# A fused attention and gated convolution: sums for two sets of scales in the free columns of the score tiles, fewer plain fp32 pairs, and a new order

## The chip, the cores and the metric

The kernel runs on one core of a Trainium2 chip. The metric is the device time of one execution in microseconds (us). The kernel before takes 588.35 us, the median of three runs (588.15 to 589.11). The core has five engines that run their own queues in order and wait for each other by semaphores: TensorE (PE, matmuls into PSUM), VectorE (DVE), ScalarE (ACT), GpSimd (POOL) and SyncE (SP, which issues the DMAs).

## The reference

```python
scores = scale * np.matmul(q, k.transpose(0, 1, 3, 2)) - np.log(S)   # q, k, v: 8 x 12 x 448 x 64
attn = 1.0 / (1.0 + np.exp(-scores))
x = np.matmul(attn, v)                           # then 8 x 448 x 768, heads side by side
gate_pre[t] = sum(conv_w[k] * xp[t + k] for k in range(5))   # xp: x with 4 zero tokens ahead
gate = 1.0 / (1.0 + np.exp(-gate_pre))
out = (gate * (x @ w_val)) @ w_out               # w_val, w_out: 768 x 768
```

All is fp32. There is no softmax: each score goes through a sigmoid alone.

## The kernel before, in words

**Units.** A *pair* is two heads of one batch (48 pairs, number i), a *two* is two pairs (24 twos, number j), and three twos are a batch. Tokens stand in the free dimension: a tile of scores has keys on its partitions and 448 queries beside each other, one half for each head. The first three chunks of 128 keys of a pair are `scores` (lines 497 to 510), the last 64 keys of both pairs of a two are one tile, `scores_rest` (512). Score tiles are `ps_a`, a ring of three PSUM buffers of two 512-wide halves, of which the scores fill columns 0 to 447. `attend` (575) multiplies the sigmoids by v, again into a `ps_a` tile, which becomes x.

**Plain and split.** A fp32 product on PE is either plain, or split into high and low parts with three cheaper matmuls (high·high and the two mixed ones). For the scores, pairs in `WHOLE_SCORES` are plain and the others have q and k split by `split_qk` (`qk_hi` by ACT or DVE, `qk_lo` by POOL). For the attend, twos in `WHOLE` are plain (`a_single`); for the others the sigmoid is written back into PSUM (line 541), ACT makes the fp16 high part `a`, DVE the low part (line 552), and v is split by a scale that is found from its maximum: a maximum on DVE (`vm`), a sum over partitions by a one-column matmul against ones (line 525), read by DVE (`v_exp`, line 533), four small DVE steps and `v_hi`, `v_lo`.

**Batches.** Batch 0's x goes to DRAM, and 64 of its tokens are appended to each of batches 1 to 7, which so have 512 tokens. For each of them: `x_max` (line 642) per two, the convolution (`gate`, 655: a first tap and four more per pair, then a sigmoid), and when its third two is done `x_scale` (664): DVE reduces `x_max`, spreads it on a 128x128 `diagonal` (673), PE sums that against ones into a `ps_m` tile (675), DVE reads it back (676) and makes a power-of-two scale, after which `x_split` makes the fp16 parts `xs`. `product` (704) makes for each of six output columns a chain of 18 fp16 matmuls of 512 columns (line 719): "val" (here V0 to V5) gives y, gated by DVE (743) and split into `g`; "out" (O0 to O5) takes the `g` and goes to the output. `ps_m` is a ring of two 512-wide PSUM buffers; two products run interleaved. One batch's O follow after the next batch's scale.

**Weights.** They come as 64-bit words and are turned into fp32 by DVE and ACT (`convert`), and then split to fp16 by `weight_split` (411): a sum of one column on PE (414) into a `ps_m` tile, small DVE steps (`exponent`, 386), a high part (361) and a low part (429) for each of 6 columns of each weight. `EARLY` = 5 columns of w_out are split while the first batch is attended, the last one with batch 1's products.

**Order.** A planner (129 to 246) takes all operations with a due time, worked out from the numbers in `AT` (74), and writes each engine's queue: of the ready operations the one with the earliest due time goes first. Chains with `then` (a pair's three chunks, an attend) stay together on PE. DVE and POOL aren't put side by side where they share an operand port.

## Time and profile before

| | us |
|---|---|
| three runs, median (lowest to highest) | 588.35 (588.15 to 589.11) |
| the profiled execution's own time | 587.99 |
| its span in the trace | 586.2 |
| PE busy in the span | 577.5 |
| DVE busy | 454.4 |
| ACT busy | 373.1 |
| POOL busy | 69.4 |

So 1.8 us of an execution lie outside the span. The busy times are sums over the whole span; how close an engine is to its limit in one stage is read from windows. The chain of waits follows the work that ended last back to the start, and each of its rows gives the start, the length and the line of one stretch on it. Start times are from the start of the span.

### The profile page before, as it was taken

Reading aid. Unit: us, or ns where it says so; the run is one execution under the profiler, and the core shown is the slowest. Engines: PE = TensorE matmul, PEld = TensorE weight load, DVE = VectorE, ACT = ScalarE, POOL = GpSimd, SP = SyncE. Lnnn points to the kernel's source line nnn. Section 1 sums busy time; section 2 is a strip of 40 time slices with the busy share of each in tenths; the row PEclk is TensorE's granted clock in tenths of the full one; section 3 lists DMA queues with packets and bytes.
Section 4 is the critical chain, followed back from the end, with each engine's and each line's share of the span. In section 5 each row is a group of like instructions: output and inputs, shape, how many; then the busy total and the mean of one; then the engine's idle time right before and its main releaser. Section 6 shows DMA issues by size and latency. Waiting matters only on the chain.

```text
span 586.2 us, 9120 instructions
## 1 busy us (share of the span) xinstructions
PE 577.5 (99%) x3509; PEld 274.6 (47%) x3509; DVE 454.4 (78%) x744; ACT 373.1 (64%) x495; POOL 69.4 (12%) x86
## 2 busy tenths in 40 slices
PE   8999999999999999999999999999999999999997
PEld 4333333444554455554545455455454544444444
DVE  1889999989978899889999789996899964813210
ACT  6678768646787677877767677687776762321111
POOL 0000020032110311112121131210111000100000
PEclk9999999999999999999999999999999999999999
DMA  8997633213232121431213322043220111021012
GB/s 314 394 335 227 215 102 123 49 61 126 53 115 71 74 96 37 130 101 47 95 25 124 90 75 66 30 130 95 67 85 0 37 42 36 2 72 37 0 37 72
DMA packets 30811, 56.94 MB, mean 97 GB/s; under 512 B 14000, under 2 KB 19632, under 8 KB 30768
## 3 DMA queue, kind: packets, MB, share of 16 engines
q1 hardware_dynamic: 30768, 56.37, 29.1%
q8 instruction: 27, 0.44, 0.3%
q14 instruction: 16, 0.13, 0.1%
HBM read 43.96 MB, written 12.40 MB: 96 GB/s over the span
## 4 chain that ended last, share of the span: by engine, by line
PE 85%; DVE 12%; ACT 2%; issue 1%; ACTq 0%; DVEq 0%
PE ps_m L719 54%; PE ps_a L506 13%; PE ps_a L599 12%; DVE gate L655 3%; PE ps_a L528 3%; PE ps_a L591 2%; DVE w_words L381 1%; ACT a_single L541 1%; DVE w_words L404 1%; DVE x_max L642 1%; DVE y L743 1%; DVE out_max L407 1%; DVE w_out_lo L429 1%; PE ps_m L766 1%; ACT y L359 1%
## 5 line engine op out<-in xcount | busy, mean ns | idle before, releaser
L719 PE MATMUL ps_m<-g,w_out_hi 128*128 128x512 f16 (+1 forms) x516 | 150.5, 374 | 1.6 <-ACT y L359 0.7
L719 PE MATMUL ps_m<-xs,w_val_hi 128*128 128x512 f16 x504 | 150.0, 379 | 1.0 <-DVE y L743 0.4
L655 DVE SCALAR_TENSOR_TENSOR gate<-x,cw,gate 128x512 f32<-128x512 f32 x168 | 123.2, 760 | 0.2
L552 DVE SCALAR_TENSOR_TENSOR a<-ps_a,a 128x896 f16<-128x896 f32 x84 | 88.9, 1084 | 12.5 <-ACT a L359 12.3
L719 PE MATMUL ps_m<-g,w_out_lo 128*128 128x512 f16 (+1 forms) x258 | 96.5, 374 | 0.0
L719 PE MATMUL ps_m<-xs,w_val_lo 128*128 128x512 f16 x252 | 95.5, 379 | 0.0
L541 ACT ACTIVATE ps_a<-ps_a 128x896 f32<-128x896 f32 x98 | 86.5, 904 | 9.5 <-DVE v_exp L533 5.9
L364 POOL TENSOR_TENSOR qk_lo<-qk_src,qk_hi 128x448 fp32r<-128x448 f32 (+1 forms) x52 | 61.8, 1209 | 249.8 <-ACT qk_hi L353 201.7
L719 PEld LDWEIGHTS <-w_val_hi 128*128 128x128 f16 x504 | 48.0, 98 | 63.6 <-issue 8.6
L719 PEld LDWEIGHTS <-w_out_hi 128*128 128x128 f16 x516 | 49.3, 98 | 60.7 <-issue 6.1
L359 ACT ACTIVATE a<-ps_a 128x896 f16<-128x896 f32 x84 | 74.3, 924 | 0.3
L359 ACT ACTIVATE y<-ps_m,o_scale 128x512 f32<-128x512 f32 (+1 forms) x39 | 26.0, 682 | 60.6 <-PE ps_m L719 59.8
L541 ACT ACTIVATE a_single<-ps_a 128x896 f32<-128x896 f32 x70 | 59.6, 924 | 7.5 <-PE ps_a L591 3.6
L743 DVE SCALAR_TENSOR_TENSOR y<-ps_m,y_scale,gate 128x512 f32<-128x512 f32 x42 | 30.1, 744 | 34.8 <-PE ps_m L719 32.6
L506 PE MATMUL ps_a<-qk_single 64*128 64x448 f32 x264 | 55.4, 554 | 0.0
L359 ACT ACTIVATE gate<-x,cw 128x512 f32<-128x512 f32 x38 | 27.6, 730 | 36.8 <-DVE y L743 36.8
L599 PE MATMUL ps_a<-a_single,v_src 128*64 128x448 f32 x240 | 47.3, 543 | 0.0
L599 PE MATMUL ps_a<-a,v_hi 128*64 128x448 f16 x336 | 46.1, 354 | 0.0
L658 ACT ACTIVATE gate<-gate 128x512 f32<-128x512 f32 x42 | 26.0, 628 | 25.2 <-DVE gate L655 25.1
L719 PEld LDWEIGHTS <-w_out_lo 128*128 128x128 f16 x258 | 25.2, 98 | 29.2
L719 PEld LDWEIGHTS <-w_val_lo 128*128 128x128 f16 x252 | 24.6, 98 | 29.8
L506 PEld LDWEIGHTS ps_a<-qk_single 64*128 64x128 f32 x264 | 23.8, 187 | 25.5 <-issue 17.1
(105 smaller groups left out, 641.0 us busy)
## 6 DMA issues: line engine op xcount, KB each, us to landing
qk_src<-qk SPq DMA_DIRECT2D x26, 448.0 KB, 3.8
v_src<-vs SPq DMA_DIRECT2D x24, 448.0 KB, 3.3
qk_single<-qk SPq DMA_DIRECT2D x21, 448.0 KB, 4.9
out_t<-y SPq DMA_DIRECT2D x41, 224.0 KB, 2.0
w_words<-w_val SPq DMA_DIRECT2D x6, 768.0 KB, 10.2
w_words<-w_out SPq DMA_DIRECT2D x6, 768.0 KB, 6.2
x<-first_x SPq DMA_DIRECT2D x21, 68.0 KB, 2.3
first_x<-x_first SPq DMA_DIRECT2D x3, 452.0 KB, 5.6
```

Source lines behind the costliest of these rows:

```text
L359: nc.scalar.activation(to, x, AF.Copy, scale=by)
L364: engines[eng].tensor_tensor(to, x, y, op=ALU.subtract)
L506: mm(b()[:, h, :S], k()[rows, at : at + P], q()[rows, :S], start=(n == 0), stop=(n == len(terms(i)) - 1))
L528: mm(b()[to, h, :S], x[n]()[rows, CW:], x[n]()[rows, :S], start=True, stop=True)
L541: nc.scalar.activation(to, b()[:, :, :S], AF.Sigmoid, bias=-math.log(S), scale=1.0 / math.sqrt(D))
L552: op({"V": 1.0}, t + 0.5, lambda e: nc.vector.scalar_tensor_tensor(part(1), p(), A_SCALE, part(0), op0=ALU.mult, op1=ALU.subtract), [b], [ ...
L591: mm(px()[to, p, :S], v()[rows, h * D : (h + 1) * D], x(s["a"])[rows, h, at : at + S], start=(n == 0), stop=False, skip_group_check=True)
L599: mm(px()[to, p, :S], v()[:, o : o + D], x(st[2 * j + p]["a", c])[:, h, at : at + S], start=False, stop=(c == 2 and n == len(parts) - 1), ...
L655: op({"V": 0.67}, at + AT["tap_step"] * k, lambda e, p=p, g=g, w=w, k=k: nc.vector.scalar_tensor_tensor(by(g()), x()[:, p, :, HALO - k : H ...
L658: op({"A": 0.55}, t + AT["gate"] + AT["tap_pair"] * p, lambda e, g=g: nc.scalar.activation(g(), g(), AF.Sigmoid), [], [g])
L719: mm(po()[:, cs], w()[:, c, :], x(k)[:, cs], start=(c == 0 and j == 0), stop=(c == NC - 1 and j == 2))
L743: op({"V": 0.66}, t + AT["y"], lambda e: nc.vector.scalar_tensor_tensor(y(), po(), y_scale()[:, m : m + 1], gate(), op0=ALU.mult, op1=ALU. ...
```

## The change

- `WHOLE` shrinks from twos 0 to 9 to twos 0 to 7, and `WHOLE_SCORES` from 22 pairs to pairs 0 to 15: twos 8 and 9 and pairs 16, 18, 19, 24, 43 and 47 become split.
- The sum for the scale of x of batches 1 to 6 no longer takes a `ps_m` tile. It stands in columns 448 to 511 of both halves of the first score chunk of the pair after the next two's first pair (pair 2j+3), as two matmuls of 64 columns ahead of the scores. Batch 7's has a `ps_a` tile of its own. The chunk's scores wait for the diagonal, and its first sigmoid (which writes the same tile) waits for DVE's read of the sum.
- Two of w_out's columns are split early (`EARLY` = 2). The sums for columns 2 to 5 stand in the free columns of the first chunk of pairs 15 and 17, two in each, and they are split after that.
- O of a batch stand in one piece ahead of the next V, `LEFT` is gone, and `weight_scales("out")` comes with batch 2.
- All numbers in `AT` are new.

The diff, with the table of numbers cut to its first line:

```diff
--- before.py
+++ after.py
@@ -36,8 +36,8 @@
 AHEAD = 2 * NP
-WHOLE = {*range(10)}
-WHOLE_SCORES = {*range(17), 18, 19, 24, 43, 47}
+WHOLE = {*range(8)}
+WHOLE_SCORES = {*range(16)}
 FIRST_SPLIT = min({*range(NPAIRS + 1)} - WHOLE_SCORES)
@@ -63,21 +63,21 @@
 WORDS = 4
-LEFT = 2
-
-EARLY = 5
+
+EARLY = 2
+LATER = 6
 BY_GPSIMD = ()
 AT = dict(
-    first=5.68, step=10.7, val=-72.5, val_step=48.7, out=-14.5, out_step=40.23, w_max=-95, w_split=-56,
...
+    first=5.14, step=12.99, val=-102, val_step=51.22, out=19, out_step=147.94, w_max=-53.5, w_split=-117,
...
 )
@@ -383,11 +383,11 @@
         op({"A": 0.06 + 0.76 * c, "V": 0.06 + 0.41 * c}, prio + 0.2, lambda e: scaled(
             e, high().bitcast(F32), high().bitcast(F32), REBIAS), [], [t])
-    def exponent(e, read, cols, prio):
+    def exponent(e, read, cols, prio, po=None):
         op({"V": 0.08}, prio, lambda _: nc.vector.tensor_scalar(
-            cols[0](), read[1](), 0x7F800000, None, op0=ALU.bitwise_and), read[0], e, port="")
+            cols[0](), read[1](), 0x7F800000, None, op0=ALU.bitwise_and), read[0], [*e, po] if po else e, port="")
         op({"V": 0.06}, prio + 0.2, lambda _: nc.vector.tensor_scalar(
             cols[0](), cols[0](), float(31 << 23), float(254 << 23), op0=ALU.max, op1=ALU.min), [], e)
         op({"V": 0.06}, prio + 0.4, lambda _: nc.vector.tensor_scalar(
@@ -408,13 +408,22 @@
             b()[:, m : m + 1], t()[:, :, 1].bitcast(F32), axis=AX.X, op=ALU.max, apply_absolute_value=True),
            [t], [b], port="")
-    def weight_split(n, m):
+    def weight_sum(n, m):
+        b = w_max[n][m]
+        return [b, ones], lambda to: mm(to[:, m : m + 1], ones(), b()[:, m : m + 1], start=True, stop=True)
+
+    def weight_split(n, m, po=None, to=None):
+
         prio = AT[n] + AT[n + "_step"] * m + AT["w_split"]
-        t, po, b = single[n, m], ps_m.new(), w_max[n][m]
-        op({"P": 0.05}, prio - 1, lambda e: mm(po()[:, :1], ones(), b()[:, m : m + 1], start=True, stop=True), [b, ones], [po])
+        t = single[n, m]
+        if po is None:
+            po = ps_m.new()
+            to = lambda: po()
+            reads, emit = weight_sum(n, m)
+            op({"P": 0.05}, prio - 1, lambda e: emit(to()), reads, [po])
         e, inv = w_scale[n][m], w_inverse[n][m]
         col, bits = (lambda b: b()[:, m : m + 1]), (lambda b: b()[:, m : m + 1].bitcast(I32))
-        exponent([inv, e], ([po], lambda: po()[:, :1].bitcast(I32)), (lambda: bits(inv), lambda: bits(e)), prio - 0.5)
+        exponent([inv, e], ([], lambda: to()[:, m : m + 1].bitcast(I32)), (lambda: bits(inv), lambda: bits(e)), prio - 0.5, po)
         op({"V": 0.06}, prio, lambda _: nc.vector.tensor_scalar(
             col(inv), col(inv), 2.0**-V_TOP, None, op0=ALU.mult), [e], [inv])
         h, l = w_hi[n, m], w_lo[n, m]
@@ -494,20 +503,23 @@
             return [st[i]["qk"], st[i]["more"]]
         return [st[i]["qk"]] if i in WHOLE_SCORES else [b for pair in st[i]["halves"] for b in pair]
-    def scores(i, c):
+    def scores(i, c, sums=()):
         b = st[i]["ps", c] = ps_a.new()
         def emit(e):
+            for _, more in sums:
+                more(b())
             for n, (k, q) in enumerate(terms(i)):
                 for h, rows in enumerate(halves):
                     at = S + c * P
                     mm(b()[:, h, :S], k()[rows, at : at + P], q()[rows, :S],
                        start=(n == 0), stop=(n == len(terms(i)) - 1))
-        cost = (0.755 if i in WHOLE_SCORES else 0.607) + (0.1 if c != 1 else 0) + (0.09 if c == 0 and i % 2 else 0)
-        return op({"P": cost}, tau(i) + AT["scores"], emit, sources(i, c), [b])
+        cost = (0.755 if i in WHOLE_SCORES else 0.607) + (0.1 if c != 1 else 0) + (0.09 if c == 0 and i % 2 else 0) + 0.06 * len(sums)
+        return op({"P": cost}, tau(i) + AT["scores"], emit,
+                  sources(i, c) + [x for reads, _ in sums for x in reads], [b])
     def scores_rest(j):
@@ -661,20 +673,29 @@
     outer = {}
-    def x_scale(b):
+    def x_largest(b):
         t = tau((b + 1) * NP) + AT["x_scale"]
-        m, d, e, po = xm[b], diagonal.new(), x_exp.new(), ps_m.new()
+        m, d, e = xm[b], diagonal.new(), x_exp.new()
         for c in range(3):
             two[3 * b + c]["xe"] = e
+        op({"V": 0.12}, t, lambda _: nc.vector.tensor_reduce(
+            e()[:, :1].bitcast(F32), m(), axis=AX.X, op=ALU.max), [m], [e], port="")
+        op({"V": 0.16}, t + 0.1, lambda _: nc.vector.tensor_scalar(
+            d(), eye(), e()[:, :1].bitcast(F32), None, op0=ALU.mult), [eye, e], [d])
+
+        def spread(to):
+            for n, cs in enumerate(halves):
+                mm(to[:, n, S : S + D], ones(), d()[:, cs], start=True, stop=True)
+
+        return [ones, d], spread
+
+    def x_scale(b, po):
+
+        t, e = tau((b + 1) * NP) + AT["x_scale"], two[3 * b]["xe"]
         col = lambda n: e()[:, n : n + 1]
-        op({"V": 0.12}, t, lambda _: nc.vector.tensor_reduce(
-            col(0).bitcast(F32), m(), axis=AX.X, op=ALU.max), [m], [e], port="")
-        op({"V": 0.16}, t + 0.1, lambda _: nc.vector.tensor_scalar(
-            d(), eye(), col(0).bitcast(F32), None, op0=ALU.mult), [eye, e], [d])
-        op({"P": 0.06}, t + 0.2, lambda _: mm(po()[:, :P], ones(), d(), start=True, stop=True), [ones, d], [po])
         op({"V": 0.22}, t + 0.3, lambda _: nc.vector.tensor_reduce(
-            col(0).bitcast(F32), po()[:, :P], axis=AX.X, op=ALU.max), [po], [e], port="")
+            col(0).bitcast(F32), po()[:, :, S : S + D], axis=AX.XY, op=ALU.max), [], [e, po], port="")
         exponent([e], ([], lambda: col(0)), (lambda: col(0), lambda: col(1)), t + 0.4)
     def x_unscale(b):
@@ -780,12 +801,14 @@
         if i not in WHOLE_SCORES:
             split_qk(i)
-    def score(i, after=None):
-        first, middle, last = (scores(i, c) for c in range(3))
+    def score(i, after=None, sums=(), then=()):
+        first, middle, last = (scores(i, c, sums if c == 0 else ()) for c in range(3))
         first.then, middle.then = middle, last
         if after:
             after[1].then = first
             after[0].deps.update(d for b in sources(i) for d in b.writers)
+        for f in then:
+            f(st[i]["ps", 0])
         for c in range(3):
             t = tau(i) + AT["a_first" if i < AHEAD else "a"] + c * 0.4
             st[i]["a", c] = attention(st[i], t, st[i]["ps", c], a_ring, "a", i // 2 in WHOLE)
@@ -819,30 +842,38 @@
             if j + 1 not in WHOLE:
                 v_scale(j + 1)
             score(2 * j + 2, (o, last))
-            score(2 * j + 3)
+            sums, then = [], []
+            if j % 3 == 2 and j > 2:
+                sums.append(x_largest(j // 3))
+                then.append(lambda b, n=j // 3: x_scale(n, b))
+            for m in range(EARLY, NC):
+                if j == LATER + (m - EARLY) // 2:
+                    reads, emit = weight_sum("out", m)
+                    sums.append((reads, lambda to, emit=emit: emit(to[:, 0, S:])))
+                    then.append(lambda b, m=m: weight_split("out", m, b, lambda: b()[:, 0, S:]))
+            score(2 * j + 3, None, sums, then)
         b = j // 3
         if j % 3 < 2:
             continue
-
-        if b > 1:
-            for m in range(NC - LEFT):
-                product("out", b - 1, m)
         if b == 0:
             weight_scales("val")
             continue
-        x_scale(b)
+        if b == B - 1:
+            reads, spread = x_largest(b)
+            po = ps_a.new()
+            op({"P": 0.12}, tau((b + 1) * NP) + AT["x_scale"], lambda e: spread(po()), reads, [po])
+            x_scale(b, po)
         for c in range(3):
             x_split(3 * b + c)
+        if b == 2:
+            weight_scales("out")
+            x_unscale(1)
         if b > 1:
-            for m in range(NC - LEFT, NC):
+            x_unscale(b)
+            for m in range(NC):
                 product("out", b - 1, m)
         for m in range(NC):
-            if b == 1 and m + EARLY < NC:
-                weight_split("out", m + EARLY)
             product("val", b, m)
-        if b == 1:
-            weight_scales("out")
-        x_unscale(b)
     for m in range(NC):
         product("out", B - 1, m)
     plan.close(rings)
```

What the change moves in the queues stands below at three places, word for word as built: a row is the line, the instruction, what it writes and reads, its size, and the semaphores that it waits for.

PE around the first sum of x (batch 1), in the kernel before: the rows after the attend of two 6 (L506 scores, L414 the sum of a w_out column, L675 the sum of x).

```order
L506 MATMUL ps_a<-qk_single 128x448 [waits Activation_49]
L506 MATMUL ps_a<-qk_single 128x448
L414 LDWEIGHTS ones
L414 MATMUL ps_m<-out_max,ones 128x1 [waits DVE_49]
L675 LDWEIGHTS ones
L675 MATMUL ps_m<-diagonal,ones 128x128
L506 MATMUL ps_a<-qk_single 128x448 [waits Activation_49]
L506 MATMUL ps_a<-qk_single 128x448
L506 MATMUL ps_a<-qk_single 128x448 [waits Activation_49]
```

PE at the same place in the kernel after: the rows after the attend of two 5 (L517 scores of pair 12, L689 the sum of x, then pair 13).

```order
L517 MATMUL ps_a<-qk_single 128x448 [waits Activation_49]
L517 MATMUL ps_a<-qk_single 128x448
L517 MATMUL ps_a<-qk_single 128x448 [waits Activation_49]
L517 MATMUL ps_a<-qk_single 128x448
L689 LDWEIGHTS ones [waits DVE_49]
L689 MATMUL ps_a<-diagonal,ones 128x64 [waits Activation_49]
L689 LDWEIGHTS ones
L689 MATMUL ps_a<-diagonal,ones 128x64
L517 MATMUL ps_a<-qk_single 128x448 x2
L517 MATMUL ps_a<-qk_single 128x448 [waits Activation_49]
```

The sum of x stands one two earlier, directly behind pair 12's scores; its weight load waits for DVE, and behind it stand pair 13's scores.

DVE around the third `x_max` of batch 1, in the kernel before (L379 and L381 convert weights, L389 to L393 and L418 are small steps for a w_out column, L671 and L673 make the diagonal, L645 copies the edges of x).

```order
L381 TENSOR_SCALAR w_words<-w_words 128x768 [waits DVE_49]
L642 TENSOR_REDUCE x_max<-x 128x2 [waits DMAHW4_49,Activation_49]
L389 TENSOR_SCALAR out_inverse<-ps_m 128x1 [waits PE_49]
L671 TENSOR_REDUCE x_exp<-x_max 128x1 [waits DVE_49]
L391 TENSOR_SCALAR out_inverse<-out_inverse 128x1 [waits DVE_49]
L673 TENSOR_SCALAR diagonal<-eye,x_exp 128x128 [waits DVE_49]
L393 TENSOR_SCALAR out_scale<-out_inverse 128x1 [waits DVE_49]
L645 COPY x<-x 128x2x6x4
L418 TENSOR_SCALAR out_inverse<-out_inverse 128x1 [waits DVE_49]
```

DVE at the same place in the kernel after (L667 gate taps, L404 a weight conversion, L657 the edges of x, L682 and L684 make the diagonal, L697 reads the sum).

```order
L667 SCALAR_TENSOR_TENSOR gate<-x,cw,gate 128x512 [waits DVE_49]
L404 SCALAR_TENSOR_TENSOR w_words<-w_words 128x768 [waits Activation_49]
L654 TENSOR_REDUCE x_max<-x 128x2 [waits DMAHW5_49,Activation_49]
L657 COPY x<-x 128x2x6x4 [waits DMAHW1_49]
L682 TENSOR_REDUCE x_exp<-x_max 128x1 [waits DVE_49]
L361 TENSOR_SCALAR gate<-x,cw 128x512
L684 TENSOR_SCALAR diagonal<-eye,x_exp 128x128 [waits DVE_49]
L667 SCALAR_TENSOR_TENSOR gate<-x,cw,gate 128x512 [waits DVE_49,Pool_49]
L407 TENSOR_REDUCE out_max<-w_words 128x1
L697 TENSOR_REDUCE x_exp<-ps_a 128x1 [waits DVE_49,PE_49]
```

The small steps of a w_out column no longer stand there; the copy of the edges and the first tap of a gate now stand between `x_max` and the diagonal.

PE at the boundary from batch 6's O4 and O5 to batch 7's first V, in the kernel before (`w_out_hi_83`, `lo_95` belong to O4, `w_out_hi_84`, `lo_96` to O5; a product's chain has six steps of three matmuls).

```order
L719 LDWEIGHTS w_out_hi_83
L719 MATMUL ps_m<-g_5190,w_out_hi_83 128x512
L719 LDWEIGHTS w_out_lo_95
L719 MATMUL ps_m<-g_5190,w_out_lo_95 128x512
L719 LDWEIGHTS w_out_hi_84
L719 MATMUL ps_m<-g_5190,w_out_hi_84 128x512
L719 LDWEIGHTS w_out_hi_84
L719 MATMUL ps_m<-g_5190,w_out_hi_84 128x512
L719 LDWEIGHTS w_out_lo_96
L719 MATMUL ps_m<-g_5190,w_out_lo_96 128x512
L719 LDWEIGHTS w_val_hi_73
L719 MATMUL ps_m<-xs,w_val_hi_73 128x512 [waits Activation_49]
```

PE at the same boundary in the kernel after (same names).

```order
L740 LDWEIGHTS w_out_hi_84
L740 MATMUL ps_m<-g,w_out_hi_84 128x512
L740 LDWEIGHTS w_out_lo_96
L740 MATMUL ps_m<-g,w_out_lo_96 128x512
L740 LDWEIGHTS w_out_hi_84
L740 MATMUL ps_m<-g_5329,w_out_hi_84 128x512
L740 LDWEIGHTS w_out_hi_84
L740 MATMUL ps_m<-g_5329,w_out_hi_84 128x512
L740 LDWEIGHTS w_out_lo_96
L740 MATMUL ps_m<-g_5329,w_out_lo_96 128x512
L740 LDWEIGHTS w_val_hi_73
L740 MATMUL ps_m<-xs,w_val_hi_73 128x512 [waits Activation_49]
```

Before, O4 and O5 end with their steps side by side, O4's last step just ahead of O5's last; after, O4 has ended and two steps of O5 follow one another before the V begin.

## Rows read from the trace of the kernel before

**Rows 1.** The page's first part: busy us, share of the span and instructions of each engine.

```profile
PE 577.5 (99%) x3509; PEld 274.6 (47%) x3509; DVE 454.4 (78%) x744; ACT 373.1 (64%) x495; POOL 69.4 (12%) x86
```

**Rows 2.** Windows: stretch, length, then busy us and instructions of each engine; PE's granted clock.

```profile
core 0: us, PE busy (x) PEld busy (x) DVE busy (x) ACT busy (x) POOL busy (x), PEclk, DMA share, GB/s
74.00:86.00 12.00, 11.96 (x71) 4.54 (x69) 12.00 (x24) 8.36 (x11) 3.27 (x2) 1.00 0.30 94
100.00:160.00 60.00, 59.71 (x349) 26.75 (x347) 55.81 (x93) 40.87 (x56) 10.77 (x12) 1.00 0.24 73
100.00:480.00 380.00, 379.52 (x2461) 188.83 (x2459) 335.93 (x526) 276.73 (x371) 62.56 (x68) 1.00 0.24 75
```

**Rows 3.** The chain of waits, middle of the span: start, length, engine, buffer, line, instructions.

```profile
106.78 0.75 PE ps_a L591 x8
107.53 4.66 PE ps_a L599 x24
...
182.46 0.57 PE ps_a L591 x12
183.03 3.53 PE ps_a L599 x36
186.56 2.46 PE ps_a L506 x12
189.01 7.88 PE ps_m L719 x36
196.89 2.02 PE ps_a L506 x18
```

**Rows 4.** The chain of waits in the last 84 us.

```profile
502.50 22.18 PE ps_m L719 x102
524.67 0.07 PE ps_m L675
...
525.11 7.30 PE ps_m L719 x33
...
533.22 7.30 PE ps_m L719 x33
...
573.94 5.75 PE ps_m L719 x33
```

**Rows 5.** Timeline of PE: start, length, instruction and, in brackets, idle time before it.

```profile
77.64 0.18 PE L414 MATMUL ps_m<-out_max,ones 128*128 128x1 bf16 x1
...
101.71 0.59 PE L719 MATMUL ps_m<-xs,w_val_hi 128*128 128x512 f16 x2 [0.29 <-DVE out_inverse L389]
```

**Rows 6.** Timeline of DVE around the second and third maximum of batch 1's x.

```profile
65.55 1.20 DVE L642 TENSOR_REDUCE x_max<-x 128x2 f32<-128x1024 f32 x1
...
77.53 1.19 DVE L642 TENSOR_REDUCE x_max<-x 128x2 f32<-128x1024 f32 x1
...
78.94 0.25 DVE L673 TENSOR_SCALAR diagonal<-eye,x_exp 128x128 bf16<-128x128 bf16 x1
```

**Rows 7.** Groups of DVE's instructions by form: busy us, mean ns of one, idle before.

```profile
L655 DVE SCALAR_TENSOR_TENSOR gate<-x,cw,gate 128x512 f32<-128x512 f32 x168 | 123.2, 760 | 0.2
L552 DVE SCALAR_TENSOR_TENSOR a<-ps_a,a 128x896 f16<-128x896 f32 x84 | 88.9, 1084 | 12.5 <-ACT a L359 12.3
L429 DVE SCALAR_TENSOR_TENSOR w_out_lo<-w_words,out_scale,w_out_hi 128x768 f16<-128x768 f32 x6 | 6.1, 1018 | 0.0
L355 DVE CAST qk_hi<-qk_src 128x448 fp32r<-128x448 f32 x8 | 3.1, 386 | 3.1 <-issue 3.1
L361 DVE TENSOR_SCALAR w_out_hi<-w_words,out_scale 128x768 f16<-128x768 f32 x5 | 3.1, 617 | 0.0
L533 DVE TENSOR_SCALAR v_exp<-ps_a 128x1 int32<-128x1 int32 x14 | 2.1, 151 | 0.5 <-PE ps_a L528 0.4
```

**Rows 8.** Timeline of PE: an O step behind DVE's read of a `ps_m` tile.

```profile
324.04 0.59 PE L719 MATMUL ps_m<-g,w_out_hi 128*128 128x512 f16 x2 [0.19 <-DVE y L361]
```

**Rows 9.** Window of the last 2 us, after PE's last matmul (columns as in rows 2).

```profile
584.00:586.00 2.00, 0.00 (x0) 0.00 (x0) 0.00 (x0) 0.00 (x0) 0.00 (x0) 0.75 0.23 66
```

More of the change, by code (lines that the diff above doesn't have):

```diff
@@ L63 @@
 WORDS = 4
-LEFT = 2
-EARLY = 5
+EARLY = 2
+LATER = 6
 BY_GPSIMD = ()
 AT = dict(
-    first=5.68, step=10.7, val=-72.5, val_step=48.7, out=-14.5, out_step=40.23, w_max=-95, w_split=-56,
-    load_qk_first=-148.5, load_qk=88.5, load_v=-126.5, split_hi=-58, split_lo=-3.5, rest_first=90.5,
-    rest=134, a_first=-125.5, a=26, attend=-48.5, v_max=-6.5, v_exp=24, v_split=-163.5, x=-221,
-    x_max=-164.5, x_scale=-272, x_hi=32, x_lo=-56, x_step=228.61, tap=42.5, scores=58, a_rest=79,
-    a_rest_first=-26, tap_pair=73, tap_step=21.64, gate=-90, product=31, y=-60.5, g_hi=113.5, g_lo=-19.5,
-    o=-46, w_load=-68,
+    first=5.14, step=12.99, val=-102, val_step=51.22, out=19, out_step=147.94, w_max=-53.5, w_split=-117,
+    load_qk_first=-107.5, load_qk=97, load_v=-114.5, split_hi=-15, split_lo=-9.5, rest_first=89,
+    rest=200.5, a_first=-125, a=5, attend=-73.5, v_max=35, v_exp=62.5, v_split=-215, x=-272.5, x_max=-95,
+    x_scale=-244.5, x_hi=86.5, x_lo=-126.5, x_step=287.31, tap=27, scores=55, a_rest=61.5,
+    a_rest_first=-31, tap_pair=84.5, tap_step=15.43, gate=-147.5, product=80, y=-44.5, g_hi=122.5,
+    g_lo=17.5, o=-107.5, w_load=-89.5,
 )
```

## The prediction

> **What bounds the kernel now.** The page's busy times come first: PE is busy for 577.5 of 586.2 us, the next engine, DVE, for 454.4 [rows 1]. An average hides stages, so the windows are next. From 100 to 480 us, where attention and products alternate, PE is busy for 379.52 of 380 us, and DVE has 44 us free; from 100 to 160 us it has only 4.2 free of 60; and from 74 to 86 us both engines are full, DVE with 12.00 and PE with 11.96 of 12 [rows 2]. So PE sets the end nearly everywhere, a microsecond of PE work saved is one saved at the end, and in the first 160 us DVE stands close enough to take over. The chain of waits says which PE work: attends, scores and pairs of products, in blocks that repeat [rows 3]. Only at the end does the chain leave PE: from 525 us on, each pair of products is followed by a wait for the copy of its result [rows 4]. These are the places where time can be won, and the first is where it can be lost.
>
> **Plain to split.** A plain attend takes 0.75 + 4.66 = 5.41 us, a split one 0.57 + 3.53 = 4.10 [rows 3]. Twos 8 and 9 change over: 2 x 1.31 = 2.6 us less PE. A pair's plain scores take 2.46 us, split ones 2.02 [rows 3]; six pairs change over: 6 x 0.44 = 2.6 less. In return each new split two asks DVE for seven low parts of 1.08 us [rows 7] and the steps for v; 47 of the casts of q and k go from ACT to DVE, at no more than 0.39 each [rows 7] some 18 us. Against that DVE sheds 17 casts of g to ACT (19 before, 2 after), which I price like the casts of q and k, 6.6 us. The net load on DVE is 14 x 1.08 + 18 - 6.6 = 27 us, some more with v; it fits into the 44 free us of the middle [rows 2] if it spreads evenly. Where it doesn't, it is the third rival's.
>
> **The tail.** Before batch 7 the two products of a pair run in step: both results are ready at the same time, both PSUM tiles are occupied, and PE waits for a copy before the next pair. From 533.22 to 573.94 us there are five such periods, 8.14 us each [rows 4]. Where the products are shifted against each other by a step, 102 matmuls take 22.18 us [rows 4], 7.83 for the 36 of a pair, since one tile is always being filled while the other is read. Before, the sum of x in a `ps_m` tile (524.67) is the point at which this shift is lost [rows 4]. After, that sum has no `ps_m` tile, and the order of PE shows the shift kept into batch 7's V, with O4 done and two steps of O5 in a row ahead of them. Six periods run so from 525.11 to 573.94 us: 48.83 - 6 x 7.83 = 1.9 us, and 0.4 between 524.67 and 525.11 less the sum itself: 2.2 us less. The bound on the other side is zero, if the shift is lost for another reason.
>
> **Sums out of `ps_m`.** Two short waits of PE behind such tiles, 0.29 us [rows 5] and 0.19 [rows 8], should go: 0.5. New small matmuls are 7 more for x and 2 more for v; at the 0.07 us that the sum of x adds to the chain [rows 4] that is 0.6 more. The four sums of w_out cost no more than before, since they are as many matmuls in another tile.
>
> **The new wait.** In the new order the first sum of x stands one two earlier, right behind pair 12's scores, and pair 13's scores stand behind it on PE. PE comes to that place at 77.64 us [rows 5], where the sum of a w_out column stands before. The diagonal, though, is ready on the kernel before only at 78.94 + 0.25 = 79.19 us [rows 6], and DVE can't be early: it is full there [rows 2]. Between the second and the third maximum it has 12.0 us of work before (65.55 to 77.53) [rows 6]. After, by its order, it has as much there: eight taps of 0.76 us instead of four, one split of a w_out column instead of two, at 1.02 + 0.62 and four small steps of about 0.15 each [rows 7]. Between the third maximum and the diagonal now stand a copy of edges and the first tap of a gate, priced below a later tap's 0.76 [rows 7], and DVE has copied an x itself. So the diagonal comes between 79.2 and 81.1 us, and PE waits between 1.6 and 3.5 us, which nothing hides: scores, attend and products all stand behind it in one queue. I take 2.8, nearer to the later end, since the added steps are in the order for certain. In before the same wait is hidden, because the sum comes one two, some 11 us, later. Starting the products earlier gives nothing back by itself, since PE had other work there.
>
> **Small waits behind a full DVE.** The first split two and the four w_out columns (9 us, at 2.2 each as above) come in the stretch from 100 to 160 us, where DVE has 4.2 us free [rows 2]. Adding DVE's rows of the new order up to the first pairs of V and to the first `v_exp`, I find it at these points between 1 us ahead of and 1 us behind PE. That bounds the loss by 0 and about 2 us; I take 0.8. The first sigmoid of a chunk that holds a sum now waits for DVE's read; PE has a pair of products of 7.88 us [rows 3] queued right behind these scores, which hides it.
>
> **The sum.** Less: 2.6 + 2.6 + 2.2 + 0.5 = 7.9. More: 0.6 + 2.8 + 0.8 = 4.2. Net -3.7 us, against the profiled execution's 587.99 (span 586.2, 1.8 outside it, which the change doesn't touch): 584.3. The median of the runs is 0.36 above that execution, so the forecast is 584.6.
>
> **Rivals.** *The first sum waits little.* Batch 1's maxima come early, because three w_out columns have left DVE before this point; then the 2.8 and part of the 0.8 go, and the time is about 581.4. For it: 2.2 us less per column. Against it: eight more taps stand ahead of the third maximum, at 0.76 about 6.1 us, as much as three columns give. Chance 0.14.
>
> *The wait also costs clock.* PE's granted clock reads 1.00 in every window of work, but 0.75 as a mean over the last 2 us, where PE has nothing to do [rows 9]: it falls below the level of 2.4 GHz when PE stands still. A wait of 3 us at 78 us could do the same, and what follows, pair 13's scores of 2.46 us [rows 3], would run at 1.2 GHz and take twice as long: +2.5, 587.1. Against it: the middle's windows all read 1.00, short waits of PE included [rows 2]. Chance 0.16. The Trainium skill says so too, on the page "TensorE: Matmul & The Clock Gate", section "HAM oscillation — how this bites in real kernels": a wait between bursts of matmuls throttles the clock, and the next burst starts slow; the trace agrees as far as the last window's 0.75 goes, and no earlier wait of this trace is long enough to test it.
>
> *DVE becomes the bound between 100 and 160 us, and the kernel gets slower.* There it has 4.2 us free [rows 2] and gets four w_out columns (9.0) and the low parts of at least one more split two (seven of 1.08 and v's, 8.7), while the eight taps that went ahead relieve it by 6.1: 9.0 + 8.7 - 4.2 - 6.1 = 7.4 more than fits, 592.0. It decides from the point where DVE's work between two readings of `v_exp` exceeds the 24 us that PE has for a two (4.10 + 2 x 2.02 + 2 x 7.88 [rows 3]). Against it: an even spread gives DVE 336 + 27 of 380 us in the middle [rows 2], and ACT takes the g casts in that stretch. Chance 0.11.
>
> *The change doesn't do what it says.* The tail keeps its period and the waits for `ps_m` come back in another place: 2.7 us less gain, 587.3. Chance 0.07.
>
> **How the numbers follow.** The forecast has 0.52. With the bounds of its unknown terms (the wait 1.6 to 3.5, small waits 0 to 2, the tail's 2.2 or part of it) its own range is 582.6 to 586.7. The range of 8 in 10 goes from 581.0, the early case, to 588.2, above the clock's case and the one without the tail; DVE's case stays outside. About 0.2%, 1.2 us, is what a measurement here can tell from no change: faster means below 587.2, slower above 589.5. Faster: 0.52 + 0.14 and most of the clock's case, 0.78; the same 0.11; slower 0.11.
>
> **What would show it.** An idle time of PE of 1.6 to 3.5 us before the first two 64-column sums near 78 us, ended by DVE's diagonal; a granted clock of 1.00 in the windows after it (below that, the clock's case); periods of 7.8 us instead of 8.1 in the last 60 us; split attends of 4.1 us from two 8 on; PE idle between 100 and 160 us below 1.5 us. The prediction is wrong if PE waits for `y` or `v_exp` again and again after 100 us, or if the first sum finds its diagonal ready.

## The result

The kernel after takes 583.45 us, the median of five runs (583.24 to 583.91), against 588.35 before: a ratio of 0.9916 with a 95% interval of 0.9905 to 0.9927. Forecast were 584.6 us, with a range of 581.0 to 588.2 and 0.78 for faster, which meant below 587.2. The profiled execution's span went from 586.2 to 581.8 us.

The page's first part of the kernel after (busy us, share, instructions), beside [rows 1]:

```profile
PE 572.3 (98%) x3586; PEld 279.4 (48%) x3586; DVE 482.4 (83%) x802; ACT 376.3 (65%) x488; POOL 82.6 (14%) x101
```

PE has 5.2 us less to do and DVE 28.0 more, where 27 were worked out. The 5.2 are not the plain and split products alone: their sets by themselves lower PE's busy time from 577.0 to 572.3 us, and the shift in the tail alone lowers it from 577.5 to 576.4 (both below). The windows that answer to [rows 2] (columns as there):

```profile
74.00:86.00 12.00, 10.76 (x66) 3.98 (x62) 11.69 (x24) 8.84 (x13) 0.50 (x1) 1.00 0.44 142
...
100.00:160.00 60.00, 59.70 (x360) 29.04 (x358) 55.98 (x104) 43.50 (x59) 14.84 (x13) 1.00 0.25 81
100.00:480.00 380.00, 379.69 (x2499) 193.59 (x2497) 353.18 (x579) 272.09 (x356) 71.18 (x77) 1.00 0.25 80
```

From 100 to 480 us PE stands still for 0.31 us in all, although DVE carries 353.18 us instead of 335.93. What PE loses, it loses before: here are all of its waits of 0.1 us or more between 20 and 480 us, from the timeline of PE (in brackets the idle time and what ended it).

```profile
55.17 1.02 PE L517 MATMUL ps_a<-qk_single 64*128 64x448 f32 x4 [1.32 <-DVE x L355]
...
59.90 0.98 PE L540 MATMUL ps_a<-qk_single 64*64 64x448 f32 x8 [1.14 <-ACT a_single L553]
...
69.21 2.63 PE L517 MATMUL ps_a<-qk_single 64*128 64x448 f32 x12 [0.20 <-ACT a_single L553]
...
81.85 0.23 PE L689 MATMUL ps_a<-diagonal,ones 128*128 128x64 bf16 x2 [1.23 <-DVE diagonal L684]
...
144.78 0.47 PE L517 MATMUL ps_a<-qk_hi 64*128 64x448 f32 x2 [0.30 <-ACT x L359]
```

The last but one is the new wait that was forecast, at the first sum of x. The first two were not forecast. (The kernel before waits there too, at 34, 46 and 57 us for 0.35, 0.38 and 0.21 us.) In the tail, the chain of waits no longer leaves PE from the sum of x of batch 7 to the last half column, where [rows 4] had a wait for each pair:

```profile
515.00 0.06 PE ps_a L689 x2
515.06 60.25 PE ps_m L740 x285
...
575.38 0.69 ACT y L359
```

The 36 matmuls of a pair now take 7.77 us, read from the timeline between the starts of two pairs (there, 24 matmuls with high and 12 with low parts of w_val lie between these rows):

```profile
531.08 0.59 PE L740 MATMUL ps_m<-xs,w_val_hi 128*128 128x512 f16 x2
...
538.85 0.59 PE L740 MATMUL ps_m<-xs,w_val_hi 128*128 128x512 f16 x2
```

### The profile page after: what moved, and what is told of

The parts are those of the page before. It is cut to its first block, busy times and chain, and to the rows that moved or that the text cites. A ratio compares the mean times of both kernels' runs of the same rounds, so it can differ in the third digit from the quotient of the medians.

```text
span 581.8 us, 9330 instructions
## 1 busy us (share of the span) xinstructions
PE 572.3 (98%) x3586; PEld 279.4 (48%) x3586; DVE 482.4 (83%) x802; ACT 376.3 (65%) x488; POOL 82.6 (14%) x101
## 4 chain that ended last, share of the span: by engine, by line
PE 85%; DVE 11%; ACT 3%; issue 1%; DVEq 0%; ACTq 0%
PE ps_m L740 54%; PE ps_a L517 13%; PE ps_a L611 12%; PE ps_a L540 3%; DVE gate L667 2%; PE ps_a L603 2%; DVE a L564 1%; DVE w_words L381 1%; ACT a_single L553 1%; DVE w_words L404 1%; DVE w_val_lo L438 1%; DVE x_max L654 1%; DVE out_max L407 1%; PE ps_m L787 1%; DVE w_words L379 0%
## 5 line engine op out<-in xcount | busy, mean ns | idle before, releaser
L667 DVE SCALAR_TENSOR_TENSOR gate<-x,cw,gate 128x512 f32<-128x512 f32 x168 | 123.3, 752 | 1.1
L364 POOL TENSOR_TENSOR qk_lo<-qk_src,qk_hi 128x448 fp32r<-128x448 f32 x64 | 70.1, 1114 | 308.6 <-DVE qk_hi L355 149.6
L564 DVE SCALAR_TENSOR_TENSOR a<-ps_a,a 128x896 f16<-128x896 f32 x96 | 101.1, 1083 | 10.4 <-ACT a L359 10.2
L553 ACT ACTIVATE ps_a<-ps_a 128x896 f32<-128x896 f32 x112 | 99.2, 906 | 8.8 <-DVE v_exp L545 4.7
L359 ACT ACTIVATE a<-ps_a 128x896 f16<-128x896 f32 x96 | 84.8, 926 | 0.1
L353 ACT CAST g<-y 128x512 f16<-128x512 f32 x40 | 24.8, 620 | 74.7 <-DVE y L764 74.2
L553 ACT ACTIVATE a_single<-ps_a 128x896 f32<-128x896 f32 x56 | 47.6, 926 | 8.4 <-PE ps_a L517 4.1
L611 PE MATMUL ps_a<-a,v_hi 128*64 128x448 f16 x384 | 52.7, 354 | 0.0
L517 PE MATMUL ps_a<-qk_single 64*128 64x448 f32 x192 | 41.5, 565 | 1.5 <-DVE x L355 1.3
L517 PE MATMUL ps_a<-qk_hi 64*128 64x448 f32 x192 | 38.8, 401 | 0.3 <-ACT x L359 0.3
L611 PE MATMUL ps_a<-a_single,v_src 128*64 128x448 f32 x192 | 37.8, 543 | 0.0
```

What stands on the lines that cost most here:

```text
L353: nc.scalar.copy(to, x)
L359: nc.scalar.activation(to, x, AF.Copy, scale=by)
L364: engines[eng].tensor_tensor(to, x, y, op=ALU.subtract)
L517: mm(b()[:, h, :S], k()[rows, at : at + P], q()[rows, :S], start=(n == 0), stop=(n == len(terms(i)) - 1))
L553: nc.scalar.activation(to, b()[:, :, :S], AF.Sigmoid, bias=-math.log(S), scale=1.0 / math.sqrt(D))
L564: op({"V": 1.0}, t + 0.5, lambda e: nc.vector.scalar_tensor_tensor(part(1), p(), A_SCALE, part(0), op0=ALU.mult, op1=ALU.subtract), [b], [ ...
```

## Experiments

### The two sets, alone and undone

The sets of plain twos and pairs were put into the kernel before, and the old sets into the kernel after.

```diff
 in the kernel before
-WHOLE = {*range(10)}
-WHOLE_SCORES = {*range(17), 18, 19, 24, 43, 47}
+WHOLE = {*range(8)}
+WHOLE_SCORES = {*range(16)}
```

> The kernel before with only the two sets changed (twos 8 and 9 and pairs 16, 18, 19, 24, 43, 47 split), old numbers in AT and old places of all sums. Theory (the two PE terms stand alone): two attends give 2.6 us, six pairs of scores 2.6, less 0.1 for two small sums: about 583.3 us, with the tail still in periods of 8.1 us. Rival (the new DVE work needs the new order): five w_out columns are still split before 100 us and the first split twos come on top, so DVE is the bound there, PE waits, and less than half of the 5.2 arrives: 586 us or more.

Measured: 621.85 us, ratio 1.0585 (1.0554 to 1.0616). That is on the rival's side, and far above the 586 us where the rival began. Its windows show PE waiting from 100 us on:

```profile
100.00:130.00 30.00, 20.84 (x137) 10.13 (x134) 27.98 (x43) 19.68 (x25) 4.94 (x4) 0.85 0.29 93
130.00:160.00 30.00, 24.76 (x158) 12.02 (x158) 28.37 (x42) 22.29 (x31) 9.00 (x11) 0.93 0.18 54
```

DVE is busy for 56.35 of these 60 us, hardly more than in the kernel before (55.81 [rows 2]) and the kernel after (55.98), where PE lost next to nothing. So a full DVE alone is not the difference. What PE waits for stands late in DVE's queue, as the low part of a sigmoid does here:

```profile
127.36 0.56 PE L506 MATMUL ps_a<-qk_hi 64*128 64x448 f32 x2 [3.18 <-DVE a L552]
```

The granted clock is a second loss: 0.85 and 0.93 as means. One wait shows it, in the timeline of PE and then in the chain and a window behind it:

```profile
206.96 1.01 PE L719 MATMUL ps_m<-g,w_out_hi 128*128 128x512 f16 x2 [4.52 <-DVE x_exp L676]
```

```profile
206.96 10.22 PE ps_m L719 x33
```

```profile
207.00:210.00 3.00, 3.00 (x8) 1.05 (x8) 2.90 (x6) 1.15 (x1) 0.00 (x0) 0.50 0.00 0
```

After 4.52 us of waiting, matmuls ran at 0.50, the lower level of 1.2 GHz, and 33 of them took 10.22 us where they take 7.30 otherwise [rows 4].

> The kernel after with the two sets as in the kernel before (ten plain twos, 22 plain pairs). Theory (the PE terms stand alone): the 5.2 us less 0.1 come back, 583.45 + 5.1 = 588.5 us, and PE's waits up to the first sum of x stay as they are. Rival (splitting costs waits elsewhere that are saved here): 586 to 587.5 us.

Measured: 588.16 us, ratio 0.9994 (0.9984 to 1.0003) to the kernel before, 4.7 us above the kernel after. So the two PE terms together are there (5.1 were expected), and all the rest of the change, new order, sums and late splitting, is worth nothing measurable as a whole. That is a balance: the tail's gain and the loss before the first products, both below, are in it. DVE now has room from 100 to 160 us (43.73 busy), and the waits at 55, 60 and 82 us stand there unchanged with 1.32, 1.14 and 1.23 us, so they don't come from the sets.

```profile
100.00:160.00 60.00, 60.00 (x315) 26.11 (x313) 43.73 (x81) 29.70 (x40) 4.33 (x4) 1.00 0.20 61
```

### The numbers that set the order

The kernel after with `AT` as in the kernel before.

```diff
-    first=5.14, step=12.99, val=-102, val_step=51.22, out=19, out_step=147.94, w_max=-53.5, w_split=-117,
+    first=5.68, step=10.7, val=-72.5, val_step=48.7, out=-14.5, out_step=40.23, w_max=-95, w_split=-56,
...
```

> The kernel after with the numbers in AT of the kernel before, all else as in the kernel after. Theory (the order spreads DVE's work, and that the kernel before with the two sets alone came to 621.85 us is the order's doing): DVE is the bound between 90 and 160 us again, PE waits for low parts and sums, products are pushed behind the last attend: 600 us or more. Rival (the later splitting of w_out and the new places of the sums are enough): 583.5 to 588 us.

Measured: 621.01 us, ratio 1.0553 (1.0538 to 1.0569). The theory's time holds, its reason only in part. The window from 110 to 160 us has PE at 34.60 of 50 us and a clock of 0.76, with PE waiting up to 4.90 us for low parts that DVE makes. But DVE is not full there, with 43.08 of 50 us: the low parts come late because DVE too waits, for ACT and for PE.

```profile
110.00:160.00 50.00, 34.60 (x231) 17.92 (x232) 43.08 (x75) 37.21 (x50) 12.70 (x15) 0.76 0.22 70
```

```profile
144.73 0.19 PE L537 MATMUL ps_a<-vm,ones 128*128 128x1 bf16 x1 [4.90 <-DVE a L564]
```

So neither the later splitting of w_out nor the new places of the sums suffice with these numbers. They were made for the old sets and the old places of the sums; whether another order near the old one could hold the new sets was not tried.

### The shift in the tail

Only PE's queue from batch 6's O4 on was changed, in the kernel before to the shifted form, in the kernel after to products in step.

```diff
 a pair of products, by steps, in the kernel before
-O4 O5 O4 O5 O4 O5 O4 O5 O4 O5 O4 O5
+O4 O4 O5 O4 O5 O4 O5 O4 O5 O4 O5 O5
```

> The kernel before with nothing changed but PE's queue from batch 6's O4 on: in every pair of products the second is shifted by one step against the first (O4 O4 O5 O4 O5 ... O5 in place of O4 O5 O4 O5 ...). Theory (products in step make PE wait for the copy of both results): periods go from 8.14 to 7.83 us, 2.2 us in all, 586.2 us. Rival (the period is set by something else than the step, such as the copies' rate or the weight loads): no change, 588.3 us.

Measured: 586.02 us, ratio 0.9956 (0.9941 to 0.9971): 2.3 to 2.5 us less by the medians, and 2.6 by the traces, counted from the sum of x of batch 7 to the end. The chain's pieces of 7.30 us with waits between them [rows 4] have become one:

```profile
524.78 0.07 PE ps_m L705
...
525.22 51.99 PE ps_m L749 x246
...
577.28 0.70 ACT y L389
```

> The kernel after with nothing changed but PE's queue from batch 6's O4 on, where the two products of a pair run in step as in the kernel before. Theory: periods go back to 8.14 us, six of them and the pair of O4 and O5: 583.45 + 2.2 = 585.7 us. Rival (the shift brings nothing): 583.5 us.

Measured: 586.59 us, ratio 0.9966 (0.9953 to 0.9979), 3.1 us above the kernel after. The chain waits for a copy after each pair again, here a period of 8.18 us:

```profile
531.51 7.30 PE ps_m L770 x33
...
538.89 0.76 DVE y L794
...
539.69 7.31 PE ps_m L770 x33
```

The step of the shift is the cause of the tail's gain, 2.3 to 3.1 us, in both kernels. The prediction named what had lost it: the sum in a `ps_m` tile. That was tried apart, with batch 7's sum alone back in such a tile.

```diff
-            po = ps_a.new()
+            po = ps_m.new()
```

> The kernel after with the sum of x of batch 7 alone back in a ps_m tile. By the queue that is built PE's products in the tail stay shifted by a step against each other. Theory (the shift sets the period, not the tile of the sum): periods of 7.8 us as in the kernel after, 583.5 us. Rival, which the prediction took for the cause (a sum in a ps_m tile costs the shift or its gain): 585.5 to 586.6 us.

Measured: 591.41 us, ratio 1.0053 (1.0038 to 1.0068), outside both. The shift stays, as the chain shows (318 matmuls in one piece of 67.37 us), so the sum's tile does not cost the shift. It costs something else:

```profile
505.76 0.57 PE L603 MATMUL ps_a<-a_rest,v_hi 64*64 64x448 f16 x8 [2.82 <-DVE a L564]
...
515.27 0.22 PE L864 MATMUL ps_m<-diagonal,ones 128*128 128x128 bf16 x1 [3.54 <-DVE diagonal L684]
```

```profile
515.49 67.37 PE ps_m L740 x318
```

`ps_m` buffers are given out in the order of the program, where the sum stands ahead of all of batch 6's O. Those 36 matmul triples, of which the kernel after runs five ahead of the last attend and six behind it while DVE works towards the diagonal, now come behind the sum. PE has nothing to put into the two waits, 6.36 us, and the attend after the first ran partly at 0.50 (5.23 us instead of 3.53). In the kernel before, `LEFT` put four of the O ahead of the sum in the program and two behind it; with a tile of the other ring O can stand in one piece. The two waits and the slower attend add up to 8.1 us, the kernel is 8.0 slower than the kernel after.

### Where the first products' delay comes from

PE's waits before the first products were taken on one at a time, in the kernel after. First the two early ones, by giving ACT the copy of two 3's x, and DVE two weight operations that stood ahead of sigmoids on ACT.

```diff
-DVE: copy of x (two 3)         ACT: scaling of w_out 1, high part of w_out 0
+ACT: copy of x (two 3)         DVE: scaling of w_out 1, high part of w_out 0
```

> The kernel after with three operations on another engine: the copy of two 3's x goes from DVE to ACT, and the scaling of w_out column 1's words and the high part of column 0, which stood ahead of sigmoids in ACT's queue, go to DVE. It takes away what PE waits for at 55 us (1.32) and 60 us (1.14). Theory (DVE's queue up to the first diagonal sets the pace, earlier waits are in its shadow): PE comes 2.4 us earlier to the first sum of x, waits there that much longer (3.6 us instead of 1.23), and the time stays at 583.5 us, a little more if a wait of that length costs clock. Rival (each wait costs by itself): 581.1 us.

Measured: 584.0 us, ratio 0.9924 (0.9909 to 0.9939). The time stays, as the theory has it, but the wait came back earlier than expected: the waits at 55 and 60 us are gone, one of 2.90 us appears at 67.73 us (the copy of two 4's x stands on ACT behind a weight scaling that waits for DVE), and the wait at the sum is 1.23 us as before. The theory's clause on the clock came true in two of the four executions: their mean granted clock is 0.997 and 0.996, and they took 584.43 and 584.75 us; the other two, with 1.000, took 583.39 (the one in the profile) and 583.58.

```profile
67.73 1.02 PE L547 MATMUL ps_a<-qk_single 64*128 64x448 f32 x4 [2.90 <-ACT x L383]
...
81.71 0.23 PE L719 MATMUL ps_a<-diagonal,ones 128*128 128x64 bf16 x2 [1.23 <-DVE diagonal L714]
```

Then the diagonal was put directly behind the third maximum, ahead of a conversion, the edges and a first tap.

```diff
 DVE's queue at the first sum
-words of w_out 3, maximum, edges, largest, first tap, diagonal, tap, maximum of w_out, read
+maximum, largest, diagonal, words of w_out 3, edges, first tap, tap, maximum of w_out, read
```

> The kernel after with a part of DVE's queue in another order: the first diagonal directly behind the third maximum, ahead of a conversion of weights, the copy of edges and a gate's first tap. Theory (that wait of 1.23 us on PE is those three operations): the diagonal is ready 1.0 to 1.2 us earlier, PE waits 0.2 us or less, and the time is 582.4 us. Rival (DVE gives the time back at the xs parts or the first y): 583.4 us.

Measured: 584.25 us, ratio 0.9928 (0.9914 to 0.9943). PE's wait fell to 0.33 us, and 1.54 us came back behind it, from a sigmoid that waits for DVE's read of the sum (the idle time of ACT, in the second fence, says so):

```profile
81.39 0.23 PE L719 MATMUL ps_a<-diagonal,ones 128*128 128x64 bf16 x2 [0.33 <-DVE diagonal L714]
...
85.61 0.98 PE L570 MATMUL ps_a<-qk_single 64*64 64x448 f32 x8 [1.54 <-ACT a_single L583]
```

```profile
84.64 2.54 ACT L583 ACTIVATE a_single<-ps_a 128x896 f32<-128x896 f32 x3 [1.48 <-DVE x_exp L727]
```

So the read was moved up too.

```diff
-maximum, largest, diagonal, words of w_out 3, edges, first tap, tap, maximum of w_out, read
+maximum, largest, diagonal, words of w_out 3, edges, read, first tap, tap, maximum of w_out
```

> As the kernel with the first diagonal moved up in DVE's queue, and DVE's read of the first sum of x moved up as well, ahead of two gate taps and a maximum of w_out. With the diagonal alone moved up, PE's wait of 1.23 us fell to 0.33, but 1.54 us came back four us later, because the sigmoid of the chunk that holds the sum waited for that read until 84.6 us. Theory (these are one chain: diagonal, sum, read, sigmoid): with both moved up neither wait is left, and the time is 0.9 us below the kernel after, 582.5 us. Rival (DVE is full, so the time comes back at the first products): 583.4 us.

Measured: 583.21 us, ratio 0.9912 (0.9897 to 0.9927). The waits are 0.34 us and none, and yet the time is that of the kernel after within the intervals. Waits of 0.21 and 0.35 us for copies of x on ACT have come up at 92 and 119 us; the rest is too small to be told from the start of an execution, which varies (below).

The first two edits together (the read in its old place), with two more copies of x moved ahead on ACT and more of DVE's work behind the diagonal:

```diff
-ACT: scaling of w_out 2, x of two 4; scaling of w_out 3, x of two 5
+ACT: x of two 4, scaling of w_out 2; x of two 5, scaling of w_out 3
-DVE: two conversions, two taps, words of w_out 3, maximum, ...
+DVE: maximum, largest, diagonal, two conversions, two taps, words of w_out 3, ...
```

> The two edits together, and besides, on ACT the copies of x of twos 4 and 5 ahead of two weight scalings that wait for DVE, and on DVE two more conversions of weights and two gate taps behind the diagonal. Theory: none of PE's three waits ahead of the first products is left, 3.3 us less, 580.2 us, if DVE makes up for what was put behind; if it does not, 581.5 us. Rival (DVE is the bound up to the first products whatever its order): 583.4 us.

Measured: 587.42 us, ratio 0.9985 (0.9975 to 0.9995), 4.0 us worse than the kernel after. The diagonal is ready at 80.5 us, but now the PSUM tile for the sum is not: its sigmoid stands on ACT behind a weight scaling, which waits for the DVE operation that was moved. At 68.85 us PE waits for 2.40 us besides, and behind the longer wait its granted clock reads 0.50, so that pair 13's scores take 4.22 us.

```profile
81.50 0.90 ACT L389 ACTIVATE w_words<-w_words 128x768 f32<-128x768 f32 x1 [2.69 <-DVE w_words L411]
```

```profile
84.29 0.22 PE L719 MATMUL ps_a<-diagonal,ones 128*128 128x64 bf16 x2 [4.03 <-ACT a_single L583]
```

None of the four orders gets the 3.5 us back. DVE is full there or nearly so (11.69 us busy of 12 from 74 to 86 us in the kernel after), ACT's queue is interlocked with it through the weights, and a wait taken from one place appears at the next. That any order would be as slow is not shown; only these were tried.

The load itself was changed by splitting five columns of w_out early, as in the kernel before.

```diff
-EARLY = 2
+EARLY = 5
```

> The kernel after with five of w_out's columns split early, as in the kernel before, and one late; the rest of the order is planned anew with the same numbers. Theory (DVE is the bound up to the first diagonal): three more columns at 2.2 us of DVE stand ahead of it, PE's waits before the first products grow by some 4 to 6 us, part of which is won back later, since DVE has less to do behind: 586 to 589 us. Rival (the early waits are ACT's order, not DVE's load): 583.5 us.

Measured: 601.83 us, ratio 1.0226 (1.0209 to 1.0243), beyond the theory, and by another mechanism. PE's wait at the first sum is 1.09 us, no longer than before. But behind the first V stands a one-column sum of w_out in a `ps_m` tile, and its maximum is still in DVE's queue:

```profile
108.41 0.16 PE L413 MATMUL ps_m<-out_max,ones 128*128 128x1 bf16 x1 [14.57 <-DVE out_max L407]
```

For 14.57 us everything that is queued on PE behind a sum of one column waits. The other numbers were not made for five columns, so this is no price of `EARLY` = 5 as such; it shows what a late sum in `ps_m` between products can cost. In the kernel after the late ones stand in score tiles.

### A longer wait and the clock

```diff
 DVE, between the largest and the diagonal of batch 1
+nc.vector.memset(idle, 0.0)
+for _ in range(8):
+    nc.vector.tensor_copy(idle, idle)
```

> The kernel after with added DVE work ahead of the first diagonal alone: one fill and eight copies of a 128x512 tile that nobody reads, about 4 us. PE's wait there grows from 1.23 us to about 5. Theory (a wait of that length costs clock, as in the kernel before with the two sets alone, where 33 product matmuls after a wait of 4.52 us took 10.22 us instead of 7.30): granted clock 0.50 for some 5 us after it, 583.45 + 4 + 2.5 = 590 us. Rival (only the wait counts): 587.5 us.

Measured: 589.42 us, ratio 1.0019 (1.0009 to 1.0028), 6.0 us above the kernel after. The wait is 5.44 us, 4.2 longer, and behind it pair 13's scores took 4.85 us instead of 2.53:

```profile
86.12 0.29 PE L696 MATMUL ps_a<-diagonal,ones 128*128 128x64 bf16 x2 [5.44 <-DVE diagonal L690]
86.33 4.85 PE L517 MATMUL ps_a<-qk_single 64*128 64x448 f32 x12
```

```profile
88.00:90.00 2.00, 2.00 (x8) 1.01 (x6) 1.75 (x6) 1.18 (x2) 0.00 (x0) 0.50 0.00 0
```

The theory holds. The clock's rival in the prediction was right in mechanism and price (2.5 us; these scores took 2.3 longer), but for a wait of 5.44 us; the real one of 1.23 us left the granted clock at 1.00. The page "TensorE: Matmul & The Clock Gate" of the Trainium skill, section "HAM oscillation — how this bites in real kernels", has waits between bursts lower the clock for the next burst; these rows agree, with 0.50 and nearly twice the time.

## Why the prediction was right, point by point

- **Plain to split: right.** 5.2 us were worked out, less 0.1 for the sums for v; undoing it cost 4.7, in which a small wait of 0.30 us is contained. The DVE load of 27 us was 28.0, and the middle held it. That the 28.0 came so near is partly luck. The rows of the two traces by form give 24.5 for the priced terms (low parts 14.4, casts of q and k 17.2, casts of g 7.1 less); of the 47 casts 35 came from ACT and 12 are new. The steps for v (7.0) and ten more first taps (4.7) came on top, and other operations left DVE.
- **The tail: right in kind, under-sized, half wrong in cause.** 2.2 us were forecast; 2.3 to 3.1 were measured for the shift, as the two exchanged queues show. Of the 2.2, 1.9 were for the shift, which is 2.6 by the traces: a pair takes 7.77 us and not 7.83, and the wait ahead of the last half columns fell from 0.50 to 0.17. The wait of 0.38 us for DVE's read of the sum (525.11) went as well, since that sum no longer stands between products in `ps_m`. That a sum in a `ps_m` tile loses the shift is refuted: with the sum put back, the products stay shifted. The sum's tile matters because it fixes where O may stand.
- **Sums out of `ps_m`: as forecast.** After 100 us no product waits 0.1 us or more for such a tile until the last half column. The seven more matmuls for x were over-sized: the first sum takes 0.17 us of PE's time in two matmuls (81.85 to 82.02), 0.14 before in one (89.20 to 89.34), so some 0.2 in all where 0.6 with the sums for v were taken.
- **The new wait: mis-sized, and in the wrong place.** 2.8 us were taken for one wait at the first sum, on the assumption that PE comes there at 77.64 us as before. PE had ended pair 12's scores only at 80.62 us, since it had lost 2.5 us at 55 and 60 us, and then waited 1.23, less than the 1.6 to 3.5 that was to show it. The diagonal was ready at 81.80 us, above the upper bound of 81.1:

```profile
56.04 1.21 DVE L654 TENSOR_REDUCE x_max<-x 128x2 f32<-128x1024 f32 x1
...
67.95 1.22 DVE L654 TENSOR_REDUCE x_max<-x 128x2 f32<-128x1024 f32 x1
...
79.82 1.23 DVE L654 TENSOR_REDUCE x_max<-x 128x2 f32<-128x1024 f32 x1
...
81.55 0.25 DVE L684 TENSOR_SCALAR diagonal<-eye,x_exp 128x128 bf16<-128x128 bf16 x1
```

  Between the second and the third maximum DVE has 11.87 us of work, about as much as before, as was worked out (there with four taps before, where the trace has three). From the third maximum to the diagonal it takes 1.98 us instead of 1.66. But the first and second maximum are 2.2 and 2.4 us later than before (53.80 and 65.55 [rows 6]), up to 0.7 of it the later start of this execution (below). From the first attend (11.44 us before, 12.13 after) to that of two 6, which are the same products but for the sums, the stage cost 3.5 us. The latter's row in the kernel before, then after:

```profile
81.13 0.98 PE L591 MATMUL ps_a<-a_single,v_src 64*64 64x448 f32 x8
```

```profile
85.37 0.98 PE L603 MATMUL ps_a<-a_single,v_src 64*64 64x448 f32 x8
```

  The step that failed is the one that noted "DVE has copied an x itself" and charged it to the diagonal alone: PE's scores needed the same PSUM tile, and ACT's sigmoids stood behind a weight scaling that waited for DVE. The trace of ACT has the latter as 4.61 us of idle time ahead of it:

```profile
54.24 0.89 ACT L359 ACTIVATE w_words<-w_words 128x768 f32<-128x768 f32 x1 [4.61 <-DVE w_words L381]
```

- **Small waits: over-sized.** 0.8 us were taken, 0.30 measured.
- **The sum.** With these sizes: the gains are 4.7 (the small wait and the sums for v are in it), 3.0 for the tail and 0.5 for waits behind `ps_m`; the losses are 3.5 before the first products and 0.2 for the sums of x. Net that is -4.5 us; measured were -4.9. The 0.4 left over is within what the medians tell apart. The terms of the forecast were off by up to 0.8 us in both directions, so that their sum came within 1.2 us is in part luck.
- **DVE as the bound: not here, and elsewhere by another path.** With the new order it did not occur: PE loses 0.30 us between 100 and 160 us. In the two kernels of 621 us PE waited for DVE's results again and again, at some 38 us against the kernel after, where 7.4 were named. The prediction priced DVE's surplus alone. But in these kernels DVE is hardly busier, or less busy, in the stretches where PE waits than in kernels that lose nothing there; its results came late. In the kernel with the sets alone, PE stands idle for 34.9 us of the span instead of 9.5, and it is busy for 584.7 us instead of 572.3, with as many products, where waits had lowered its clock. Neither loss was in the price.

## What to carry to other kernels

Moving work from the full engine to the next one is worth its price only together with an order made for it: here the same sets gave 4.7 us in the new order and cost 33 in one made for other sets, while the rest of the change without them gave nothing that can be measured. A pair of accumulations in two PSUM buffers should run shifted, not in step, so that one is read while the other fills (here 7.77 us a pair instead of 8.14 to 8.18). And where an in-order engine gets a new operation, look at what stands behind it that a third engine needs: three of the waits here were sigmoids or copies of x stuck on ACT behind a weight scaling that waited for DVE.

## What was not expected of the hardware

- **The length of a wait alone did not decide the clock.** After waits of PE of 4.03, 4.52 and 5.44 us the windows read 0.50. After 2.90 us (`x` on ACT), 3.32 (the sets alone, at 95.13) and 3.54 (the last sum in `ps_m`, at 515.27) they read 1.00, but after 2.82 in the tail of the kernel with the last sum in `ps_m`, and after 3.18 with the sets alone, they read 0.50. In this order:

```profile
68.00:70.00 2.00, 1.80 (x11) 0.56 (x11) 1.96 (x5) 2.00 (x4) 0.00 (x0) 1.00 0.00 0
...
97.00:99.00 2.00, 2.00 (x12) 0.81 (x14) 1.93 (x7) 1.97 (x3) 1.97 (x2) 1.00 0.72 210
...
515.00:517.00 2.00, 1.73 (x9) 0.83 (x9) 2.00 (x7) 0.00 (x0) 0.00 (x0) 1.00 0.00 0
...
508.00:510.00 2.00, 2.00 (x14) 1.02 (x12) 0.56 (x1) 0.00 (x0) 0.00 (x0) 0.50 0.00 0
...
129.00:131.00 2.00, 1.66 (x5) 0.56 (x4) 2.00 (x3) 0.00 (x0) 0.00 (x0) 0.50 0.00 0
```

  Nor did one kernel always do the same: with x on ACT, two executions of four have a lower mean clock and took about 1 us longer. Only the first of the four is traced, so at which wait the others lost it is not shown.
- **The start of an execution varies by up to 0.7 us, and by more up to the first attend.** In kernels whose PE and ACT queues are equal there, the first score matmuls ended at different times: ACT's first sigmoid started at 5.61 us in the kernel before, at 6.31 in the kernel after, and between these or with them in the others, while the granted clock read 1.00 in all. The first attend started between 11.43 and 12.52 us. The DMA queues of the kernels before and after differ there, but the orders of the kernel after alone spread from 5.77 to 6.31 us. Differences of some tenths between two profiles belong to that.
